# Attention in doubles of two head pairs: tail keys in eight 64x32 tiles, tanh written to SBUF, whole-width loads

## The chip, the core and the metric

The kernel runs on one core of a Trainium2 chip (trn2). A core has five engines with queues of their own: TensorE (PE, with its weight loads shown as PEld), VectorE (DVE), ScalarE (ACT), GpSimd (POOL, here only zeros, ones and stores) and SyncE (SP, which issues loads). They meet through semaphores. SBUF is the working memory of 128 partitions; PSUM, into which PE writes, has eight banks. The metric is the device time of one execution in microseconds (us); less is better.

## What is computed

The reference, cut to what matters (batch 4, 12 heads, 448 positions, head size 64; d_model 768, d_ff 2048; all in fp32):

```python
scores = cap * tanh(q @ k.T / sqrt(64) / cap)          # per batch and head, 448x448
attn = exp(scores - max) / (sum(exp(scores - max)) + 1e-9)
x = heads_side_by_side(attn @ v)                       # 1792 x 768
for w_in, w_out in ((moe_w_in, moe_w_out), (moe2_w_in, moe2_w_out)):
    h = maximum(x @ w_in, 0)
    x = (h * h) @ w_out
```

## The kernel before

The program has two stages. **Attention** works on 24 pairs of heads (batch b, pair j, two heads e = 0, 1), in the order of `PAIRS`. **Four passes** then do the two layers, two batches at a time (passes 0 and 1 layer one, 2 and 3 layer two), as products of 2x2 blocks with seven products instead of eight (names A11, A12, S3, S2, S1, S4, A22). A pass has 56 chunks of six 128x128 weight tiles; per tile three PE products run (L674 to L676: high and low part of weight and input). Each chunk needs its weights loaded (`wf`, issued by SP), their high part (`wh`, ACT) and low part (`wl`, DVE); there are three buffers of each.

In between, DVE and ACT prepare the weights: the inputs are float64 words, which `round_words` turns into float32 one unit at a time (load `ww`, scaled on ACT at L217, then shift L220, low bits L223, sign L226 on DVE; POOL stores `w32`); after two units four block sums (L249) are made and stored in `sums`. This work is spread over attention and passes by due times, at a rate per place (`room`).

Scores stand with keys on partitions and queries along the row. The 448 keys of a head are three tiles of 128 and a rest of 64. A **round** below is a group of matmuls that fill the array side by side. Of one pair:

- scores: three rounds (L336), each of two 64x128 matmuls, one per head, in the two row halves of the array; and one for the rest (L330): four 128x32 matmuls over both heads, where the input `qk` holds zeros so that each head sees its own half;
- ACT: tanh in PSUM (L348) and exp to SBUF (L352), in `GROUPS` of three blocks, three blocks and the rest: 1344, 1344 and 448 columns;
- sums of the weights: two rounds (L382, `ones` as the stationary operand) into bank 7; DVE turns them (L392), adds eps (L399), takes reciprocals (L400) and spreads them (L404);
- values: four rounds (L372) of four 128x32 matmuls into bank 6; DVE multiplies by the reciprocals (L422) into `m` (kept, batches 0 and 1, then split by `bring` into the `xc` slots, ACT line L474) or `o` (stored to memory, batches 2 and 3).

Scores use banks 0 to 2 and 3 to 5 in turn. PE's order in a pair is: scores of pair n, sums and values of pair n-1, rest of pair n. A pair's inputs come by five DMAs: `raw` (two of 64 partitions, three buffers) and `vr` (three; 576 columns that hold a column block of ones beside each head's values, and two strips of 16 KB; three buffers).

The order of every engine is fixed when the program is written: `Plan.emit` is a list scheduler that holds costs, places (one place is 3.66 us of PE time), due times and rings of buffers, and each engine then runs its list in that order, waiting where it has to.

## Time and profile before

| what | us |
|---|---|
| median of 3 runs (1045.92 to 1048.86) | 1046.26 |
| the profiled execution | 1043.62 |
| its span (first to last instruction) | 1041.9 |
| PE busy in the span (98%) | 1019.5 |
| DVE busy (80%) | 834.3 |
| ACT busy (67%) | 698.8 |
| first matmul of attention | 4.70 |
| first matmul of pass 0 | 201.18 |

The profiled execution's own time is 1043.62 us, 1.7 us more than its span and 2.6 us less than the median. The last two lines divide the span: 4.7 us of start, 196.5 us of attention, 840.7 us of passes and last stores.

### The profile page before, as it was taken

The numbers are of one execution on the slowest core, as the hardware profiler recorded it, in microseconds if no ns is written. First come the engines' busy times: TensorE is split into PE (matmuls) and PEld (weight loads), VectorE is DVE, ScalarE is ACT, GpSimd is POOL, SyncE is SP. The second block draws the span as 40 slices with busy tenths as digits, with TensorE's granted clock in tenths as the row PEclk, the third lists the DMA queues.
The fourth block names the chain that finished last, engine by engine and source line by source line (L and its number), as shares of the span: only waits on it lengthen the run. The fifth ranks groups of instructions, "written<-read, shape, count | busy, mean of one in ns | idle before, by whom it ended". The sixth has DMA issues, their size and how long they took to land.

```text
span 1041.9 us, 16113 instructions
## 1 busy us (share of the span) xinstructions
PE 1019.5 (98%) x5664; PEld 826.9 (79%) x5664; DVE 834.3 (80%) x1204; ACT 698.8 (67%) x963; POOL 106.6 (10%) x185
## 2 busy tenths in 40 slices
PE   7999999899999999999999999998999999999997
PEld 3333333499899989899999998987999999999996
DVE  3789877778899999887999988778997865589751
ACT  7999999587786655676965557777565444465541
POOL 0101122112111011111100111210100000000000
PEclk9999999999999999999999999999999999999999
DMA  8989999889885686899746958886646533334341
GB/s 211 295 239 271 294 273 343 287 291 292 287 271 162 211 313 222 279 311 298 252 137 219 320 195 291 269 264 210 185 136 225 155 110 110 106 110 126 116 141 63
DMA packets 107498, 231.59 MB, mean 222 GB/s; under 512 B 17105, under 2 KB 62417, under 8 KB 107409
## 3 DMA queue, kind: packets, MB, share of 16 engines
q1 hardware_dynamic: 92688, 171.88, 55.1%
q0 software_dynamic: 14720, 58.60, 15.2%
q8 instruction: 46, 0.75, 0.3%
q14 instruction: 44, 0.35, 0.1%
HBM read 166.33 MB, written 64.09 MB: 221 GB/s over the span
## 4 chain that ended last, share of the span: by engine, by line
PE 91%; DVE 3%; DMA 2%; ACT 1%; issue 1%; SPq 0%; DVEq 0%; ACTq 0%
PE bank L676 25%; PE bank L674 25%; PE bank L675 25%; PE bank L372 6%; PE bank L336 5%; PE bank L382 3%; PE bank L330 1%; DMA wf<-si 1%; DMA ww<-wout_dram 1%; DVE wl L189 1%; DVE xc L189 1%; ACT bank L348 1%; ACT p L352 0%; DVE wg L223 0%; DMA raw<-qk_dram 0%
## 5 line engine op out<-in xcount | busy, mean ns | idle before, releaser
L676 PE MATMUL bank<-xc,wl 128*128 128x448 f32 x1344 | 493.1, 367 | 6.8 <-DVE wl L189 6.8
L674 PE MATMUL bank<-xc,wh 128*128 128x448 f32 x1344 | 492.8, 367 | 1.2 <-ACT one L693 1.2
L675 PE MATMUL bank<-xc,wh 128*128 128x448 f32 x1344 | 492.5, 366 | 0.0
L607 ACT ACTIVATE wh<-wf 128x768 fp32r<-128x768 f32 x224 | 187.8, 842 | 175.0 <-PE bank L675 146.0
L676 PEld LDWEIGHTS bank<-xc,wl 128*128 128x128 f32 x1344 | 252.9, 188 | 30.8 <-DVE wl L189 9.0
L189 DVE TENSOR_TENSOR wl<-wf,wh 128x768 fp32r<-128x768 f32 x224 | 212.0, 953 | 80.6 <-ACT wh L607 79.7
L674 PEld LDWEIGHTS bank<-xc,wh 128*128 128x128 f32 x1344 | 252.9, 188 | 24.4 <-ACT one L693 1.6
L675 PEld LDWEIGHTS bank<-xc,wh 128*128 128x128 f32 x1344 | 252.9, 188 | 21.7
L693 ACT ACTIVATE one<-bank 128x448 f32<-128x448 f32 x132 | 71.1, 539 | 63.4 <-PE bank L676 58.5
L348 ACT ACTIVATE bank<-bank,caps 128x1344 f32<-128x1344 f32 (+1 forms) x72 | 79.3, 1102 | 9.1 <-PE bank L336 7.0
L352 ACT ACTIVATE p<-bank,caps 128x1344 f32<-128x1344 f32 (+1 forms) x72 | 81.6, 1133 | 2.2
L695 DVE TENSOR_TENSOR one<-bank,one 128x448 f32<-128x448 f32 x96 | 59.0, 621 | 27.2 <-PE bank L676 23.2
L372 PE MATMUL bank<-p,vr 128*32 128x448 f32 x768 | 76.6, 539 | 0.8 <-DVE o L422 0.8
L217 ACT ACTIVATE wg<-ww 128x768 f32<-128x768 f32 (+1 forms) x68 | 58.7, 866 | 17.3 <-DMA ww<-wout_dram 10.6
L336 PE MATMUL bank<-raw 64*128 64x448 f32 x288 | 64.7, 570 | 5.4 <-DMA raw<-qk_dram 4.7
L372 PEld LDWEIGHTS bank<-p,vr 128*32 128x32 f32 x768 | 24.9, 110 | 48.3 <-issue 44.0
L223 DVE SCALAR_TENSOR_TENSOR wg<-ww,wg 128x768 uint32<-128x768 uint32 (+1 forms) x68 | 61.8, 908 | 1.7
L226 DVE SCALAR_TENSOR_TENSOR wg<-ww,wg 128x768 uint32<-128x768 uint32 (+1 forms) x68 | 61.6, 906 | 1.4
L336 PEld LDWEIGHTS bank<-raw 64*128 64x128 f32 x288 | 28.3, 192 | 41.0 <-issue 22.3
L220 DVE TENSOR_SCALAR wg<-wg 128x768 uint32<-128x768 uint32 (+1 forms) x68 | 36.1, 530 | 15.7 <-ACT wg L217 15.7
L189 DVE TENSOR_TENSOR xc<-ga,xc 128x896 fp32r<-128x896 f32 (+1 forms) x50 | 45.5, 917 | 2.4 <-ACT xc L535 2.3
L382 PE MATMUL bank<-p,ones 128*32 128x448 f32 x384 | 41.1, 545 | 1.8 <-ACT p L352 1.8
(80 smaller groups left out, 815.7 us busy)
## 6 DMA issues: line engine op xcount, KB each, us to landing
wf<-si SPq DMA_DIRECT2D x120, 192.0 KB, 4.3
ww<-wout_dram SPq DMA_DIRECT2D x24, 768.0 KB, 7.4
wf<-wi SPq DMA_DIRECT2D x96, 192.0 KB, 3.8
ww<-win_dram SPq DMA_DIRECT2D x64, 192.0 KB, 5.9
wi<-wg POOLq DMA_DIRECT2D x32, 384.0 KB, 6.0
si<-wg POOLq DMA_DIRECT2D x32, 384.0 KB, 4.7
ww<-win_dram SPq DMA_DIRECT2D x16, 768.0 KB, 6.5
wf<-so SPq DMA_DIRECT2D x32, 384.0 KB, 3.5
```

What stands on the lines that cost most here:

```text
L189: nc.vector.tensor_tensor(out, a, b, op=ALU.subtract)
L223: nc.vector.scalar_tensor_tensor(m["fu"], m["t"][:, :n, 0], 29, m["fu"], op0=ALU.logical_shift_right, op1=ALU.bitwise_or)
L336: nc.tensor.matmul(groups_of[n][gi]["s"][:, at], lhsT=stk["t"][rows, S + 128 * t:S + 128 * t + 128], rhs=stk["t"][rows, :S], start=True, s ...
L348: nc.scalar.activation(s["s"], s["s"], AF.Tanh, scale=rcap)
L352: nc.scalar.activation(s["p"], s["s"], AF.Exp, scale=capt)
L372: nc.tensor.matmul(bank[32 * z:32 * z + 32, 6, :S], lhsT=vt["t"][:, w:w + 32], rhs=weights(n, t, e), start=t == 0, stop=t == 3)
L382: nc.tensor.matmul(bank[32 * z:32 * z + 32, 7, :S], lhsT=ones[:, 1 + e if t == 3 else 0], rhs=weights(n, t, e), start=half == 0, stop=half ...
L607: nc.scalar.activation(m["hi"], m["f"], AF.Copy)
L674: nc.tensor.matmul(a, lhsT=hi, rhs=x(0), start=first and z == 0, stop=False, skip_group_check=more)
L675: nc.tensor.matmul(a, lhsT=hi, rhs=x(1), start=False, stop=False, skip_group_check=more)
L676: nc.tensor.matmul(a, lhsT=lo, rhs=x(0), start=False, stop=final and z == len(xs) - 1, skip_group_check=more)
L693: nc.scalar.activation(m[g, i, n], a, AF.Copy)
```

## The change

Pairs are taken two at a time, as 12 **doubles** (u = 0, 1). Per double:

- scores: six rounds of two 64x128 matmuls (now L354; cells of two banks: 0-1, 2-3, 4-5), and one round for the rests of both pairs (L361): eight 64x32 matmuls, one per pair, head and 32 keys, in both row halves and all four column strips of the array. Each column strip writes one bank from one row half and another bank from the other; each of the two banks is written from both row halves, at different partitions;
- ACT: tanh from PSUM to SBUF (L367), 896 columns, seven times; exp in place in SBUF (L373) over 2, 2 and 3 rounds (1792, 1792, 2688 columns). The weights of a double are one tile of seven rounds, `pe` for even and `p` for odd doubles;
- sums: four rounds (L416) into one of the score cells; one turn (L426), six small operations (L431, L434, L435) and one spread of 896 columns (L439) on DVE;
- values: six rounds (L393) of four 128x32 matmuls into banks 6 and 7, and one round (L405) of eight 64x32 for the rests; one multiplication of 896 columns (L458).

`raw` is one DMA of 128 partitions per pair (four buffers). `vr` is 448 columns without the ones, by four DMAs in runs of 512 and 256 bytes (four buffers). The first units' `ww` load is one DMA instead of four. The scaling of units due in attention moves from ACT to DVE (L228). The block A21 of the rounded weights, which only the branch for a wide `cap` reads, is no longer stored; that branch makes it itself. The `wf`, `wh` and `wl` buffers take the space of `pe` and are opened after double 10's last values (`open_w`). The rates at which units are spread over the passes change (`RATES`).

```diff
-GROUPS = [[("A", 0), ("B", 0), ("A", 1)], [("B", 1), ("A", 2), ("B", 2)], [("R", 3)]]
-PARTS = [(slice(32 * r, 32 * r + 32), slice(32 * z, 32 * z + 32)) for z, r in enumerate((0, 2, 1, 3))]
+KV = 448
+EXPS = {None: [(0, 2), (2, 4), (4, 7)], 0: [(0, 1), (1, 3), (3, 5), (5, 7)], 11: [(0, 2), (2, 4), (4, 6), (6, 7)]}
...
-STEP = 2.14
-T0 = -STEP * (len(PAIRS) + 0.7)
+DOUBLES = len(PAIRS) // 2
+STEP = 3.76
+T0 = -STEP * (DOUBLES + 0.62)
+SWITCH = 0
+RATES = (1.5, 1.7, 0.5, 1.2, 0.8, 1.6)
+IN = 1.05
-URGENT = 2.0
+URGENT = 0.5
...
-    w_hi = [wp.tile([128, KC, 128], F32R, name=f"wh{i}") for i in range(3)]
-    w_f = [wp.tile([128, KC, 128], F32, name=f"wf{i}") for i in range(3)]
-    w_lo = [wp.tile([128, KC, 128], F32R, name=f"wl{i}") for i in range(3)]
+    even = ExitStack()
+    p_even = even.enter_context(tc.tile_pool(name="pe", bufs=1)).tile([128, 7, 2, S], F32, name="pe")
+    w_f, w_hi, w_lo = [], [], []
...
-            for rows, own in PARTS if l == g == 0 else [(slice(0, 128), slice(0, 128))]:
-                nc.sync.dma_start(to[own], src[rows])
+            nc.sync.dma_start(to, src)
+
+        on_act = t0 > SWITCH
...
-            nc.scalar.activation(m["ff"], m["t"][:, :n, 1].bitcast(F32), AF.Copy, scale=2.0 ** -112)
+            words = m["t"][:, :n, 1].bitcast(F32)
+            if on_act:
+                nc.scalar.activation(m["ff"], words, AF.Copy, scale=2.0 ** -112)
+            else:
+                nc.vector.tensor_scalar(m["ff"], words, 2.0 ** -112, None, op0=ALU.mult)
...
-            nc.gpsimd.dma_start(w32[l, g, i][:, :, c0:c1], m["f"][:, :2 * (c1 - c0)].rearrange("p (h c) m -> p h c m", h=2))
+            h0 = int(lower_half)
+            nc.gpsimd.dma_start(w32[l, g, i][:, h0:, c0:c1], m["f"][:, h0 * (c1 - c0):2 * (c1 - c0)].rearrange("p (h c) m -> p h c m", c=c1 - c0))
...
+        lower_half = i >= (HC if g else HF)
...
+    def open_w():
+        even.close()
+        pool = ctx.enter_context(tc.tile_pool(name="w2", bufs=1, reuse_waits="tile"))
+        for to, n, dt in ((w_f, "wf", F32), (w_hi, "wh", F32R), (w_lo, "wl", F32R)):
+            to.extend(pool.tile([128, KC, 128], dt, name=f"{n}{i}") for i in range(3))
+
     def attention():
-        groups_of, vt_of, stk_of = [], [], []
-        v_of = [qkp.tile([128, VL], F32, tag=f"vr{i}", name="vr", bufs=1) for i in range(3)]
+        p_of = [p_even, pp.tile([128, 7, 2, S], F32, tag="p", name="p", bufs=1)]
+        v_of = [qkp.tile([128, KV], F32, tag=f"vr{i}", name="vr", bufs=1) for i in range(4)]
...
+                raw["t"] = qkp.tile([128, QW], F32, tag="raw", name="raw", bufs=4)
+                nc.sync.dma_start(raw["t"], qk[b, 2 * j:2 * j + 2].rearrange("h r w -> (h r) w")[64:192])
+
+            def load_v():
+                t, src = v_of[vt["at"][0]], v[b, j]
+                nc.sync.dma_start(t[:, 64:320].rearrange("p (t w) -> p t w", w=128), src[:, 128:512].rearrange("p (t w) -> p t w", w=192)[:, :, :128])
+                nc.sync.dma_start(t[:, :384].rearrange("p (t w) -> p t w", w=64)[:, 0:6:5], src[:, :576].rearrange("p (t w) -> p t w", w=64)[:, 0:9:8])
+                for e in range(2):
+                    nc.sync.dma_start(t[half(e ^ u), 384:], src[half(e), 576 + 192 * e:640 + 192 * e])
+        def scores(k, r, place, cost):
...
+                at = cell[0]
+                if r < 6:
+                    t, w = raw_of[k, us[0]]["t"], S + 128 * (r % 3)
...
+                        nc.tensor.matmul(bank[:, at + e, :S], lhsT=t[half(e), w:w + 128], rhs=t[half(e), :S], start=True, stop=True)
+                    return
+                for u in us:
+                    t = raw_of[k, u]["t"]
+                    for z in range(4):
+                        e = z // 2 ^ u
+                        w = S + 384 + 64 * e + 32 * (z % 2)
+                        nc.tensor.matmul(bank[32 * z:32 * z + 32, at + u, :S], lhsT=t[half(e), w:w + 32], rhs=t[half(e), :S], start=True, stop=True)
+
+            o = pe(cost, emit, place, [raw_of[k, u]["done"] for u in us], take=[("sc", cell)], drop=["raw"] * 2 if r == 6 else [])
+            due = start(k) + 0.45 * r
+
+            def tanh():
+                nc.scalar.activation(p_of[k % 2][:, r], bank[:, cell[0]:cell[0] + 2, :S], AF.Tanh, scale=rcap)
+
+            p_set[k, r] = op("ACT", 978, tanh, due, [o], take=[f"p{k % 2}{r}"], drop=[("sc", cell)])
+
+        def exps(k, lo, hi, due):
+            def exp():
+                nc.scalar.activation(p_of[k % 2][:, lo:hi], p_of[k % 2][:, lo:hi], AF.Exp, scale=capt)
...
+        def values(k, r, place, cost, first, final, **more):
...
+                    e, h = z // 2, z % 2
+                    w = 128 * t + 64 * e + 32 * h
+                    nc.tensor.matmul(bank[32 * z:32 * z + 32, 6 + u, :S], lhsT=vt_of[k, u]["t"][:, w:w + 32], rhs=p_of[k % 2][:, r, e],
+                                     start=first, stop=final, skip_group_check=True)
+
+            return reads(k, [r], emit, place, cost, [vt_of[k, u]["done"]], **more)
+
+        def tails(k, place, cost, first, **more):
             def emit():
+                for u in range(2):
+                    for z in range(4):
+                        e, h = z // 2, z % 2
+                        rows = half(e ^ u)
+                        w = 384 + 32 * h
+                        nc.tensor.matmul(bank[32 * z:32 * z + 32, 6 + u, :S], lhsT=vt_of[k, u]["t"][rows, w:w + 32], rhs=p_of[k % 2][rows, 6, u],
+                                         start=first, stop=not first, skip_group_check=True)
+
+            return reads(k, [6], emit, place, cost, [vt_of[k, u]["done"] for u in range(2)], **more)
...
+                        z = 2 * e + u
+                        rhs = p_of[k % 2][:, 3 * u + t, e] if t < 3 else p_of[k % 2][:, 6, u]
+                        nc.tensor.matmul(bank[32 * z:32 * z + 32, cell[0], :S], lhsT=ones[:, 0 if t < 3 else 1 + (e ^ u)], rhs=rhs,
+                                         start=first, stop=final, skip_group_check=True)
...
+                nc.vector.tensor_scalar(m["q"], t.unsqueeze(1).to_broadcast([128, 2, S // 32]), eps, None, op0=ALU.add)
+                for z in range(4):
+                    to, own = (slice(32 * y, 32 * y + 32) for y in (z, z ^ 1))
+                    nc.vector.tensor_scalar(m["q"][to, 1 - z % 2], t[own], eps[own], None, op0=ALU.add)
...
+                nc.vector.tensor_tensor(to, bank[:, 6:8, :S], r["r"], op=ALU.mult)
...
+        def order(k):
+            new, old = [("S", r) for r in range(7)] if k < DOUBLES else [], []
+            V, D = [("V", r) for r in range(6)], [("D", t) for t in range(4)]
+            if k == 0:
+                return new
+            if k == 1:
+                return new[:2] + V[:3] + new[2:3] + V[3:] + D[:3] + new[3:] + [("T", 0), D[3]]
+            if k == DOUBLES:
+                return V[:2] + V[3:5] + D[:2] + [V[2], V[5]] + D[2:] + [("T", 0)]
+            return new[:3] + D + new[3:] + [("T", 0)] + V
...
+                if k - 1 == last - 1:
+                    pe(0, open_w, at, drop=[(n, [i]) for n in ("wf", "wh", "wl") for i in range(3)])
...
-                room += 0.5 * (1.5 if at_place < 0 else 1.4 if at_place % 56 < 28 else 0.6)
+                room += 0.5 * RATES[0 if at_place < 0 else min(int(at_place // 28) + 1, 5)]
...
-        plan.emit({"ww0": 1, "ww1": 1, "wg": 4, "wf": 3, "wh": 3, "wl": 3, "sc": [0, 3], "pv": 1, "p3": 4, "p1": 2,
-                   "raw": 3, "vr": 3, "d": 1, "y": 2, "dn": [7], "rn": 2, "o": 3, "m0": 1, "m1": 1,
+        plan.emit({"ww0": 1, "ww1": 1, "wg": 4, "wf": [], "wh": [], "wl": [], "sc": [0, 2, 4], "pv": 1, **{f"p{e}{r}": 1 for e in range(2) for r in range(7)},
+                   "raw": 4, "vr": 4, "d": 1, "y": 2, "rn": 1, "o": 2, "m0": 1, "m1": 1,
...
```

PE's list, from the middle of attention (x counts matmuls; `p`, `pe`: the weights exp(tanh)). Before, one pair:

```order
L330 MATMUL bank<-raw 32x448 x4
L336 MATMUL bank<-raw 128x448 x6
L382 MATMUL bank<-p,ones 32x448 x8
L372 MATMUL bank<-p,vr 32x448 x16
L330 MATMUL bank<-raw 32x448 x4
```

and now, one double:

```order
L354 MATMUL bank<-raw 128x448 x6
L416 MATMUL bank<-pe,ones 32x448 x16
L354 MATMUL bank<-raw 128x448 x6
L361 MATMUL bank<-raw 32x448 x8
L405 MATMUL bank<-pe,vr 32x448 x8
L393 MATMUL bank<-pe,vr 32x448 x24
```

A pair had 10 rounds, so two had 20; a double has 18, and it goes from one shape of tile to another five times instead of four.

ACT's list there. Before, a rest and the six blocks of the next pair, with one split of `bring` and one scaling of weights between:

```order
L348 ACTIVATE bank<-bank,caps 128x448
L352 ACTIVATE p<-bank,caps 128x448
L474 ACTIVATE xc_211<-m_228 128x448
L348 ACTIVATE bank<-bank,caps 128x3x448
L352 ACTIVATE p<-bank,caps 128x1344
L348 ACTIVATE bank<-bank,caps 128x3x448
L352 ACTIVATE p<-bank,caps 128x1344
L217 ACTIVATE wg_230<-ww_234 128x768
```

and now, one double's tanh and exp and the start of the next:

```order
L367 ACTIVATE pe<-bank,caps 128x896 x2
L373 ACTIVATE pe<-pe,caps 128x1792
L367 ACTIVATE pe<-bank,caps 128x896 x2
L373 ACTIVATE pe<-pe,caps 128x1792
L367 ACTIVATE pe<-bank,caps 128x896 x3
L373 ACTIVATE pe<-pe,caps 128x2688
L367 ACTIVATE p<-bank,caps 128x896 x2
```

Two pairs were 12 instructions, a double is 10, over the same 12,544 columns; no scaling of weights is left between them.

DVE's list where attention ends. Before, the first two low parts of weights (`wl`) stand ahead of the last three pairs' sums:

```order
L422 TENSOR_TENSOR o<-bank,rn 128x448
L189 TENSOR_TENSOR wl_242<-wf_239,wh_236 128x768
L189 TENSOR_TENSOR wl_243<-wf_240,wh_237 128x768
L392 STREAM_TRANSPOSE tn<-bank 128x448
L399 SCALAR_TENSOR_TENSOR dq<-tn,eps 64x14 x2
L400 RECIPROCAL dq<-dq 128x14
```

and now:

```order
L458 TENSOR_TENSOR o<-bank,rn 128x896
L240 SCALAR_TENSOR_TENSOR wg_233<-ww_235,wg_233 128x768
L243 SCALAR_TENSOR_TENSOR wg_233<-ww_235,wg_233 128x768
L228 TENSOR_SCALAR wg_230<-ww_234 128x512
L237 TENSOR_SCALAR wg_230<-wg_230 128x512
L240 SCALAR_TENSOR_TENSOR wg_230<-ww_234,wg_230 128x512
L243 SCALAR_TENSOR_TENSOR wg_230<-ww_234,wg_230 128x512
L195 TENSOR_TENSOR wl_1667<-wf_1661,wh_1664 128x768
L426 STREAM_TRANSPOSE tn<-bank 128x448
L195 TENSOR_TENSOR wl_1668<-wf_1662,wh_1665 128x768
```

The turn of the last double's sums stands behind the first low part, and that behind the first load of `wf`.

## Rows read from the trace of the kernel before

**Rows 1.** Busy time by stretch (start:end us, length, engines, PEclk, DMA share, GB/s).

```profile
26.00:170.00 144.00, 144.00 (x1254) 50.97 (x1246) 117.01 (x224) 138.07 (x140) 19.74 (x36) 1.00 0.98 283
201.00:1035.00 834.00, 826.00 (x4034) 757.58 (x4031) 682.87 (x914) 515.77 (x777) 77.20 (x123) 1.00 0.65 211
```

**Rows 2.** Chain that ended last, in attention (start us, us, what; xN rows).

```profile
20.73 2.46 PE bank L336 x12
23.19 1.64 PE bank L382 x16
24.83 3.01 PE bank L372 x32
27.84 0.75 PE bank L330 x8
...
169.98 2.48 PE bank L336 x12
```

**Rows 3.** The same chain at the start of attention.

```profile
4.70 3.37 PE bank L336 x6
8.09 1.36 ACT bank L348
```

**Rows 4.** PE in order of time where pass 0 begins.

```profile
201.18 0.47 PE L674 MATMUL bank<-xc,wh 128*128 128x448 f32 x1
```

**Rows 5.** ACT in 20:170 by shape (count, busy us, mean ns, idle before us).

```profile
L352 ACT ACTIVATE p<-bank,caps 128x1344 f32<-128x1344 f32 x38 | 52.5, 1383 | 1.1
L348 ACT ACTIVATE bank<-bank,caps 128x1344 f32<-128x1344 f32 x38 | 51.3, 1351 | 2.2 <-PE bank L336 2.2
L352 ACT ACTIVATE p<-bank,caps 128x448 f32<-128x448 f32 x19 | 12.1, 635 | 0.6
L348 ACT ACTIVATE bank<-bank,caps 128x448 f32<-128x448 f32 x19 | 11.5, 606 | 2.1 <-PE bank L330 2.1
L474 ACT ACTIVATE xc<-m 128x448 fp32r<-128x448 f32 x15 | 8.3, 567 | 0.0
```

**Rows 6.** ACT in order of time (start us, us of one, instruction).

```profile
163.86 1.35 ACT L348 ACTIVATE bank<-bank,caps 128x1344 f32<-128x1344 f32 x1 [0.39 <-PE bank L336]
165.25 1.38 ACT L352 ACTIVATE p<-bank,caps 128x1344 f32<-128x1344 f32 x1
166.52 1.35 ACT L348 ACTIVATE bank<-bank,caps 128x1344 f32<-128x1344 f32 x1
```

**Rows 7.** DVE in 20:170 by shape (columns as in rows 5).

```profile
L392 DVE STREAM_TRANSPOSE tn<-bank 128x448 f32<-128x448 f32 x19 | 12.3, 646 | 17.2 <-PE bank L382 13.7 <-ACT p L352 3.5
...
L220 DVE TENSOR_SCALAR wg<-wg 128x768 uint32<-128x768 uint32 x17 | 9.3, 547 | 0.4 <-ACT wg L217 0.4
L399 DVE SCALAR_TENSOR_TENSOR dq<-tn,eps 64x14 f32<-64x14 f32 x38 | 9.1, 240 | 0.9
...
L422 DVE TENSOR_TENSOR m<-bank,rn 128x448 f32<-128x448 f32 x12 | 7.4, 621 | 2.6 <-PE bank L372 2.4
```

**Rows 8.** DMA: one queue's packets (MB, share), issues (count, KB, us to landing).

```profile
q1 hardware_dynamic: 92688, 171.88, 55.1%
...
wf<-si SPq DMA_DIRECT2D x120, 192.0 KB, 4.3
...
raw<-qk_dram SPq DMA_DIRECT2D x48, 240.0 KB, 5.1
...
vr<-v_dram SPq DMA_DIRECT2D x24, 288.0 KB, 5.1
...
vr<-v_dram SPq DMA_DIRECT2D x48, 16.0 KB, 4.6
```

**Rows 9.** Chain that ended last, at the end of attention (columns as in rows 2).

```profile
176.29 9.09 DMA wf<-si
```

**Rows 10.** Groups by line, the whole span (columns as in rows 5).

```profile
L189 DVE TENSOR_TENSOR wl<-wf,wh 128x768 fp32r<-128x768 f32 x224 | 212.0, 953 | 80.6 <-ACT wh L607 79.7
L607 ACT ACTIVATE wh<-wf 128x768 fp32r<-128x768 f32 x224 | 187.8, 842 | 175.0 <-PE bank L675 146.0 <-issue 20.5 <-ACT xc L535 3.3
```

## What the change should do to the time

> **What bounds the kernel now.** First the busy time by stretch [rows 1]: from 26 to 170 us, inside attention, PE is busy for all of 144.00 us, ACT for 138.07 and DVE for 117.01. From 201 to 1035 us, the passes, PE is idle for 8.0 of 834 us. PE sets the time in both stages, so a gain has to come from less PE work in attention, and ACT, at 96%, stands close behind. Next the chain in order of time [rows 2]. Of one pair it holds three score rounds in 2.46 us, two sum rounds in 1.64, four value rounds in 3.01 and the rest in 0.75: 7.86 us. The next such 2.46 begins 149.25 us later after 19 pairs, so a pair takes 7.855 us and nothing but PE is in it. A value round is 3.01 / 4 = 0.7525 us. Three of these would be 2.26, and two 1.505: the change of tile shape into the scores costs 0.20 us and the one into the sums 0.135; between sums and values, of one shape, it costs nothing. Ten rounds and 0.335 us are the pair. Attention runs from 4.70 to 201.18 us [rows 3, 4], 196.5 us: 24 pairs are 188.5, and 8.0 go to filling and draining.
>
> **The steady double.** Two pairs cost 15.71 us. A double has 18 rounds, 13.545 us, and five changes of shape: values to scores 0.20, scores to sums 0.135, sums to scores 0.20, and two that the trace doesn't show, into and out of 64x32. For these I take 0.135 each, the row for going into a shape 32 columns wide; the ends are 0 (sums to values) and 0.20. Sum: 0.805, a double 14.35 us (14.08 to 14.48), 1.36 less than two pairs. This takes an eight-tile round at the price of a four-tile one. The trace shows two row halves at once (the scores) and four column strips at once (the values), each at 0.75 a round, and never both; the other bounds are under the rivals.
>
> The Trainium skill, TensorE: Matmul & The Clock Gate, section Measured speedup vs the span model, would make eight tiles one matmul's time plus some 4 ns a tile: by it, an estimate, 0.03 us more a round and under 1 us in all. No run here shows it.
>
> **Does ACT hold 14.35?** A tanh of 896 columns lies between 606 ns at 448 and 1351 at 1344: 978 [rows 5]. An independent instruction starts 1.27 us after one of 1.38 us, a dependent one 1.39 after one of 1.35 [rows 6], so the pitch of tanh is 0.90 and exp pays 0.03 for waiting. Exp is 1.76 us for 1792 columns and 2.51 for 2688, on the line through 635 and 1383. Sum: 7 x 0.90 + 2 x 1.76 + 2.51 + 0.1 = 12.4 us. The 15 splits [rows 5] at 0.49 net come three to a double in five doubles: 13.9. Exp and tanh of one size differ there by 0.03, which is the price I see for writing SBUF instead of PSUM; on all ten instructions it makes 14.2 in those five doubles. ACT fits, and only just. Within a double the walk is: S0 to S2 end at 2.5 us, the sums take a cell when the first tanh is done at 2.0, end at 5.6, the turn frees that cell at 6.4; S3 to S5 end at 8.1 and S5 wants that cell at 7.3; the rests want the cell of the fourth tanh, done at 7.6, at 8.1. The slack is 0.9 and 0.5 us. DVE stands at 81% [rows 1]; per double it loses 5.3 us of two pairs' small work (646, two at 240 and a reciprocal of the same 14 columns, 646 for the spread, 621) and gets 4.3 (646, six small ones at 240, and two of 896 columns, 1.1 each) [rows 7]. The scaling that it takes over is 0.55 a unit, by the like step, at 17 units in 11 doubles, 0.9. That cancels the gain, and ACT, which gave it up, no longer waits for `ww`. SP's list gets six fewer issues for the first units and three more a double for `vr`; bytes fall: two pairs moved 960 KB of `raw`, 640 of `vr` and 17 units in 150 us of 1536 KB each (768 read, 384 stored as `w32`, 384 of sums), 4330 KB; a double moves 960, 448 and 1.55 units of 1440, 3630 KB, or 259 GB/s against the 283 of rows 1.
>
> **Start.** One `raw` DMA of 240 x 2 KB instead of two [rows 8]; the first half's matmuls stood at 4.70, and I put the first round at 5.3. The first two rounds took 3.37 us [rows 3], so the first now ends at 6.7 and tanh begins at 6.8, 1.3 earlier than before. From there ACT is the bound: double 0 (four exps) takes 12.7 us, to 19.5. Of double 1 the two first rounds wait for cells until 17.8, then nine rounds and a score round keep PE to 25.8, while ACT has run dry at 23.9; S3 ends at 26.7, ACT needs 8.3 us more to finish double 1, at 35.0, and PE, held by the cells, starts double 2 at 33.1. Its sums want a cell that the next tanh frees at 36.0, 0.4 late.
>
> **End.** Doubles 2 to 11: 33.1 + 0.4 + 10 x 14.35 = 177.0. The last step is 11 rounds and one change, 8.4 us, to 185.4. Now the weights: their first load can't start before 177.0, since its space is `pe`. SP's issue 0.7, a load of 4.3 (median) or 9.1 us (the one on the chain) [rows 8, 9], `wh` 0.84, `wl` 0.95 [rows 10]: 183.8 or 188.6. The first is hidden by the last step, the second is 3.2 late and also holds the last turn on DVE, behind `wl`. At 4.3 it costs nothing, and the row is nearer to it, since `ww` traffic is no denser; I add 0.5. Pass 0 begins at 185.9 instead of 201.2: **15.3 us**.
>
> **Passes.** PE's list is the same there, and 8.0 us of idleness [rows 1] are what can change. DVE's and ACT's weight work is laid out anew: 21 units ahead of the first chunk instead of 18, so less in pass 0, but runs of about 9 us of DVE work between two `wl` (a chunk is 3.66) stand now at chunk 27 and near 31, 114 and 116, as they did at 48, 60 and 139. I count 0, with -6 and +6 as ends. A21's stores save only DMA.
>
> Sum against the profiled execution: 1043.6 - 15.3 = 1028.3. That execution is 2.6 below the median, so **1031** for a median.
>
> **Rivals.** (a) *The eight tiles don't run at once.* For: no row shows it, and each bank of such a round is written from both row halves. If the round falls into two groups of four, it costs 0.75 more, twice a double: 18.1 us in twelve, and the gain is gone: 1049, 0.26% over before. If only the low halves of one group meet the high halves of the other, 0.376 once a double, 4.5 us: 1035. Against: each strip writes two different banks, as the score rounds do.
>
> The Trainium skill, TensorEngine Tiling (Array Packing), section Gotcha 1: PSUM Pressure, speaks against this change: different row tiles cannot access one PSUM bank at the same time. By it the time would be that of the two groups. The trace has only rounds that keep to the rule, so no row weighs it.
>
> (b) *DMA takes PE's place, and the time is over that of before.* Its place is 26 to 180 us, where the DMA share is already 0.98 [rows 1]. `vr` goes from 512 packets a double to 1280. A packet of the issuing queue takes 0.551 x 16 x 1041.9 / 92688 = 0.099 us of one engine [rows 8]; at that price 768 more are 4.7 us of all sixteen, and the double, 0.98 x 15.71 x 3630 / 4330 = 12.9 now, would need 17.6 us: 12 x 3.3 = 39 more, 1070. It binds from 30 ns a packet and makes the kernel slower than before from 57. What fails then is `ww`: DVE's list waits for it ahead of a turn, the turn holds a cell, PE stops. Against: a strip of 64 short packets lands in 4.6 us beside 5.1 for 288 KB [rows 8].
>
> (c) *Attention gains, the passes give most of it back.* The late load (3.2), ACT a little over in five doubles (2) and three more DVE runs of 9 us (6): 1042. For: DVE is busy for 82% of the passes. Against: before had such runs too.
>
> **How the numbers follow.** A measurement can tell 0.3%, 3.1 us, from no change. Chances: the forecast 0.70, by itself 1023 to 1038; (a) 0.09, half of it in each form; (b) 0.07; (c) 0.14. Range 1021 to 1043: below, -6 in the passes, both changes of shape free (-2.7) and a start 1 us shorter; above, (c). Outside are (a) in full, (b), and a rest at both ends. Faster by over 0.3% (under 1043.1): 0.70, half of (a), most of (c), less a rest: 0.86. Within: (a) in full and the end of (c), 0.07. Slower: (b), 0.07.
>
> **What would show it.** In the profile after, the chain should hold score rounds 14.3 to 14.5 us apart, six 64x32 rests in 0.75 to 0.8 us; over 1.1 means (a). PE idle inside attention with `tn` or `ww` as releaser means (b). Pass 0 should begin near 186 us with less than 1 us of waiting for `wl`; the idle time of PE in the passes should be 2 to 14 us. Were the pitch of tanh 1.18 us or more, (14.35 - 12.4) / 7 over my 0.90, PE would wait for ACT in every double, and the forecast would be wrong by its own ACT term.

## The result, and the profile after

Nine executions of the changed kernel have a median of 1037.55 us (1031.2 to 1044.27), nine of the kernel before on the same chip 1046.36. The ratio is 0.991, with a 95% interval of 0.9883 to 0.9936: faster, 6.5 us above the forecast of 1031 and inside its range. The profiled execution took 1032.11 us (span 1030.3), 11.5 less than that of before.

The starts of the passes' 4032 matmuls divide this. A distance from one start to the next of over 0.6 us is a gap, one of 0.24 to 0.6 us a slow matmul, and the rest is steady; of the first two, what is over 203 ns is counted.

| stretch | before | after | difference | predicted |
|---|---|---|---|---|
| up to the first matmul of pass 0 | 201.18 | 193.97 | -7.2 | -15.3 |
| passes, steady | 822.3 | 817.5 | -4.8 | 0 |
| passes, slow matmuls | 2.6 | 2.6 | 0 | 0 |
| passes, gaps of PE | 9.1 | 9.6 | +0.5 | 0, from -6 to +6 |
| behind the last matmul's start, and around the span | 8.4 | 8.4 | 0 | 0 |

So half of attention's gain is missing, and there is one that nobody had forecast. The table holds for the two profiled executions; in a second trace of the changed kernel (run again, below) the steady part is 824.9 us, 2.6 more than before, so the 4.8 is not the kernel's in every execution. The chain of one steady double of after, which answers to [rows 2]:

```profile
51.45 2.46 PE bank L354 x12
53.91 3.14 PE bank L416 x32
57.05 2.46 PE bank L354 x12
59.51 0.91 PE bank L361 x16
60.42 0.75 PE bank L405 x16
61.17 4.65 PE bank L393 x48
65.82 2.46 PE bank L354 x12
```

A double takes 65.82 - 51.45 = 14.37 us (forecast 14.35), and nothing but PE is in it. The value rests, eight 64x32 tiles, take 0.75 us, what four tiles take; the score rests take 0.91, with 0.16 for the change of shape. Work by stretch, which answers to [rows 1], with two lines of the page on DMA (the last 11 us of the second stretch lie behind the passes' last matmul, at 1023.73, so its idle time is not that of the gaps):

```profile
26.00:170.00 144.00, 140.42 (x1304) 48.39 (x1304) 125.47 (x225) 130.35 (x114) 23.76 (x39) 0.99 0.78 254
201.00:1035.00 834.00, 814.36 (x3999) 751.39 (x3997) 683.49 (x910) 512.50 (x773) 73.88 (x121) 0.99 0.63 204
450.00:600.00 150.00, 150.00 (x742) 139.00 (x741) 136.93 (x174) 101.73 (x151) 17.48 (x31) 1.00 0.73 243
```

```profile
DMA packets 114919, 222.92 MB, mean 216 GB/s; under 512 B 22480, under 2 KB 73744, under 8 KB 114832
q1 hardware_dynamic: 101136, 169.52, 52.6%
```

In attention ACT has room now (130.35 of 144, from 138.07), DVE is at 87%, and the DMA share fell from 0.98 to 0.78 although the issuing queue moves 8448 packets more [rows 8]. Below, step n is PE's work from the first score round of double n to that of double n + 1, and the last step is what follows the values of double 10. Now the start, as PE went through it, and the DVE row behind which DVE's work piles up (it has no pause from there to 40.7 us):

```profile
28.17 1.02 PE L354 MATMUL bank<-raw 64*128 64x448 f32 x4 [0.36 <-ACT p L367]
30.89 1.75 PE L361 MATMUL bank<-raw 64*32 64x448 f32 x16 [1.69 <-ACT p L367]
32.38 1.75 PE L405 MATMUL bank<-pe,vr 64*32 64x448 f32 x16
34.06 0.97 PE L416 MATMUL bank<-pe,ones 128*32 128x448 f32 x8
34.97 2.90 PE L354 MATMUL bank<-raw 64*128 64x448 f32 x12
...
44.12 1.02 PE L354 MATMUL bank<-raw 64*128 64x448 f32 x4 [1.40 <-DVE tn L426]
```

```profile
27.86 0.56 DVE L228 TENSOR_SCALAR wg<-ww 128x768 f32<-128x768 f32 x1 [7.07 <-DMA ww<-win_dram]
```

and the end, with the DVE rows of that time below it:

```profile
176.34 4.72 PE L393 MATMUL bank<-pe,vr 128*32 128x448 f32 x48
183.69 4.91 PE L393 MATMUL bank<-p,vr 128*32 128x448 f32 x32 [2.63 <-DVE o L458]
188.41 1.69 PE L416 MATMUL bank<-p,ones 128*32 128x448 f32 x16
```

```profile
181.48 0.56 DVE L228 TENSOR_SCALAR wg<-ww 128x768 f32<-128x768 f32 x1 [0.31 <-DMA ww<-wout_dram]
182.07 0.56 DVE L237 TENSOR_SCALAR wg<-wg 128x768 uint32<-128x768 uint32 x1
182.55 1.08 DVE L458 TENSOR_TENSOR o<-bank,rn 128x896 f32<-128x896 f32 x1
```

Two waits that weren't in the sum: at 44.12 for a turn, and at 183.69 for the product of the double before, since the last step begins with value rounds, which want its banks; that product stood on DVE's list behind two unit steps, the first of which waited for its load. The wait of 1.69 us for tanh, at 30.89, was in the sum: the prediction let PE be held by the cells up to 33.1. But this gap and that of 2.63 us are paid twice. The windows of that time (the last three columns are granted clock, DMA share, GB/s):

```profile
31.00:33.00 2.00, 2.00 (x24) 0.57 (x32) 1.93 (x4) 0.97 (x2) 0.89 (x1) 0.50 0.57 120
33.00:35.00 2.00, 2.00 (x26) 0.21 (x10) 1.93 (x4) 1.97 (x2) 0.40 (x1) 0.71 0.93 280
...
184.00:186.00 2.00, 2.00 (x16) 0.56 (x12) 1.46 (x2) 0.00 (x0) 1.26 (x3) 0.58 1.03 392
186.00:188.00 2.00, 2.00 (x16) 0.64 (x12) 0.85 (x2) 0.80 (x1) 0.33 (x1) 0.56 1.04 388
```

Behind the gaps of 1.69 and 2.63 us PE ran at or near 0.50, the level of 1.2 GHz: the rests took 1.75 us in place of 0.98, four value rounds 4.91 in place of 3.2.

### The profile page after: what moved, and what is told of

It reads as the page before. It is cut to its first block, busy times and chain, and to the rows that moved or that the text cites. A ratio compares the mean times of both kernels' runs of the same rounds, so it can differ in the third digit from the quotient of the medians.

```text
span 1030.3 us, 15832 instructions
## 1 busy us (share of the span) xinstructions
PE 1001.5 (97%) x5664; PEld 819.5 (80%) x5664; DVE 839.4 (81%) x1191; ACT 676.6 (66%) x918; POOL 105.9 (10%) x179
## 4 chain that ended last, share of the span: by engine, by line
PE 90%; DVE 4%; DMA 4%; issue 1%; SPq 0%; POOL 0%; ACT 0%; DVEq 0%; POOLq 0%
PE bank L751 25%; PE bank L749 25%; PE bank L750 25%; PE bank L393 5%; PE bank L354 4%; PE bank L416 3%; DMA ww<-win_dram 1%; DVE wg L272 1%; PE bank L361 1%; PE bank L405 1%; DMA ww<-wout_dram 1%; DMA raw<-qk_dram 1%; DMA si<-wg 1%; DMA wo<-wg 1%; DVE wl L195 0%
## 5 line engine op out<-in xcount | busy, mean ns | idle before, releaser
L354 PE MATMUL bank<-raw 64*128 64x448 f32 x288 | 64.7, 578 | 8.4 <-DMA raw<-qk_dram 4.8
L354 PEld LDWEIGHTS bank<-raw 64*128 64x128 f32 x288 | 26.5, 194 | 46.0 <-issue 25.5
L367 ACT ACTIVATE p<-bank,caps 128x896 f32<-128x896 f32 x42 | 40.3, 998 | 11.2 <-PE bank L354 10.1
L367 ACT ACTIVATE pe<-bank,caps 128x896 f32<-128x896 f32 x42 | 40.3, 1002 | 7.7 <-PE bank L354 7.7
L226 ACT ACTIVATE wg<-ww 128x768 f32<-128x768 f32 (+1 forms) x45 | 38.0, 847 | 6.1 <-DMA ww<-wout_dram 4.1
L195 DVE TENSOR_TENSOR xc<-gb,xc 128x448 fp32r<-128x448 f32 (+1 forms) x52 | 38.7, 763 | 2.0 <-ACT xc L610 1.2
L272 DVE TENSOR_TENSOR wg<-wg,wg 128x384 f32<-128x384 f32 (+1 forms) x68 | 36.3, 534 | 2.2
L373 ACT ACTIVATE p<-p,caps 128x1792 f32<-128x1792 f32 (+2 forms) x19 | 37.0, 1949 | 0.6
```

The source lines that it names most:

```text
L195: nc.vector.tensor_tensor(out, a, b, op=ALU.subtract)
L354: nc.tensor.matmul(bank[:, at + e, :S], lhsT=t[half(e), w:w + 128], rhs=t[half(e), :S], start=True, stop=True)
L367: nc.scalar.activation(p_of[k % 2][:, r], bank[:, cell[0]:cell[0] + 2, :S], AF.Tanh, scale=rcap)
```

## The experiments

Times are medians; ratios are against the kernel before, run with them.

**Again** (no edit).

> The changed kernel once more, with no edit, since its times lie 13 us apart where those of the kernel before lie 5 apart. If the spread is in the first or the last doubles (waits for a `ww` load, and slow rounds behind them), this trace has pass 0 beginning at another time than 193.97 us, and the passes as long as in the trace shown (829.8 us from their first matmul to their last). If it is in the passes, pass 0 begins within 0.5 us of 193.97 and the sum of PE's gaps there, 10.3 us, changes instead. Either way a steady double is 14.37 us.

Median 1033.16 us, ratio 0.9872 (0.9836 to 0.9909). The profiled execution took 1041.61. Its windows:

```profile
31.00:33.00 2.00, 2.00 (x40) 0.55 (x38) 1.90 (x5) 1.73 (x2) 0.24 (x1) 1.00 1.01 249
```

```profile
450.00:600.00 150.00, 150.00 (x727) 136.27 (x727) 134.21 (x170) 102.10 (x151) 17.06 (x31) 1.00 0.73 243
750.00:900.00 150.00, 150.00 (x742) 139.13 (x741) 109.53 (x148) 74.37 (x109) 0.00 (x0) 1.00 0.47 146
```

Both halves of the expectation fell. Pass 0 began at 192.54, 1.4 earlier: after the same wait of 1.7 us the clock stayed at 1.00 this time. The gaps were as before (9.7 us). What differs is the steady part, 824.9 against 817.5 us: 727 matmuls in 150 us instead of 742, that is 206.67 ns apart (mean over hundreds of starts), up to the gap at 637 us but for 12 us from 298 on, and 202.67 from there on. Slow matmuls take another 3.5 us; most of them stand 373 to 374 ns apart behind a gap, as from 637 to 642 us, where the granted clock is 0.50. So this execution lost its 9.5 us in the steady part and the slow matmuls; PE's gaps don't show it, and the granted clock of the steady part is 1.00. The other executions left no trace; that the long ones among them lose their time in the same way is likely, and not shown.

**Rest4**: the eight tiles undone in one place.

```diff
-lhsT=t[half(e), w:w + 32], rhs=t[half(e), :S]
+lhsT=t[:, w:w + 32], rhs=t[:, :S]
```

> The eight 64x32 matmuls of the last 64 keys become eight 128x32, so that two follow each other in each column strip (they contract over the rows of both heads, so those scores are not the reference's). This undoes the eight tiles at once in one of the two places and nothing else. Theory: the round of eight costs what a round of four costs, so the edit costs one round of 0.75 us a double, with the changes of shape 0.6 to 0.95: a double of 15.0 to 15.3 us, and 12 doubles are 7 to 11 us slower than the changed kernel. Rival: the eight tiles run as two groups of four already, and nothing changes (a double of 14.37).

```profile
55.66 2.46 PE bank L354 x12
58.12 1.64 PE bank L361 x16
...
70.92 2.46 PE bank L354 x12
```

The rests take 1.64 us instead of 0.91, the double 70.92 - 55.66 = 15.26, 0.89 more. Median 1041.64, ratio 0.9957 (0.9937 to 0.9978); against the unedited kernel of again, run beside it (0.9872), that is by the ratios 8.9 us more, within the 7 to 11 expected. Eight tiles in the two halves and four strips do run at once; one such round is worth 0.89 us a double, and two at that price, an estimate, are 1.78, more than the whole 1.36 that a double gained.

**Sums_first**: the last step begins with sums (in PE's lists V stands for a value round, D for a sum round, T for the value rests, `new` for the score rounds).

```diff
-return V[:2] + V[3:5] + D[:2] + [V[2], V[5]] + D[2:] + [("T", 0)]
+return D[:3] + V + D[3:] + [("T", 0)]
```

> The order of PE's last step alone: three sum rounds, then the six value rounds, the last sum round and the rests, in place of value rounds first. Theory on the end: in the changed kernel the first value round of the last step waits 2.63 us for the product of the double before (its banks), and the clock granted after that gap is near half for four rounds, 1.9 us. With three sum rounds in front, 2.3 us of other work cover the gap: under 0.7 us of waiting, rounds at 0.75 us, and pass 0 begins 3.5 to 4.5 us earlier, near 190 us. Rival: the weights of pass 0 are late too (`wl` ends at 190.3 us), or the last turn and the last product are what pass 0 needs: it begins no earlier than 192.

```profile
183.15 4.72 PE L393 MATMUL bank<-p,vr 128*32 128x448 f32 x48 [0.40 <-DVE o L458]
...
189.55 0.44 PE L749 MATMUL bank<-xc,wh 128*128 128x448 f32 x1
...
191.89 0.70 PE L751 MATMUL bank<-xc,wl 128*128 128x448 f32 x1 [1.70 <-DVE wl L195]
```

The gap is covered, the clock holds, and pass 0 begins 4.4 us earlier than in the first trace of after and 3.0 earlier than in the second. The starts differ too; from the first scores of double 11 to pass 0 it takes 23.50 us here (from 166.05), 27.35 and 27.17 in the two traces, so the end itself gains 3.7 to 3.9. But the median is 1042.94 us, ratio 0.9942 (0.9919 to 0.9965): the third matmul waits for `wl`, which stands behind the last turn on DVE, and two more gaps come at 283 and 290 us (3.0 and 1.1 us), behind a `ww` load of 9.8 us and a `wf` load of 4.9. The gain was as expected, and the passes took 10 us more than in the first trace of after.

**Step1**: score round 3 goes ahead of six others in the second step.

```diff
-return new[:2] + V[:3] + new[2:3] + V[3:] + D[:3] + new[3:] + [("T", 0), D[3]]
+return new[:2] + V[:3] + new[2:4] + V[3:] + D[:3] + new[4:] + [("T", 0), D[3]]
```

> The order of PE's second step alone: score round 3 of double 1 goes ahead of value rounds 3 to 5 and the three sum rounds. Theory on the start: ACT ran dry for 2.83 us there, since that score round stood behind six other rounds; PE then waited 1.69 us for tanh, and the granted clock fell to 0.50 for the next rounds, some 1.5 us more. With the round ahead ACT goes on, the gap goes and the clock stays at 1.00: step 2 begins at 31 to 32 us instead of 34.97. If DVE's list, whose units stand ahead of the first turn and wait for a `ww` load until 27.9 us, doesn't come in its place, step 3 begins 3 to 4 us earlier than 51.4; the rival is that it does, with the turn at about 34 us as the releaser of PE's next gap, and step 3 begins at 49.5 to 51.4.

```profile
30.61 0.99 PE L361 MATMUL bank<-raw 64*32 64x448 f32 x16 [0.36 <-ACT p L367]
...
33.17 2.53 PE L354 MATMUL bank<-raw 64*128 64x448 f32 x12
36.25 3.21 PE L416 MATMUL bank<-p,ones 128*32 128x448 f32 x32 [0.56 <-ACT pe L367]
```

The wait of 1.69 us is 0.36; step 3 begins at 48.16, 3.2 us earlier than in the first trace of after and 2.0 earlier than in the second. No turn was waited for; the `ww` load, which DVE's list awaits ahead of the first turn, landed at 25.2 us here, and at 27.9 and 26.9 in the two traces of after. Step 2 began at 33.17, later than expected: the rounds behind the first gap, at 17 us, were slow here (three value rounds 3.42 us for 2.46). Median 1034.35, ratio 0.9894 (0.9856 to 0.9932). The unedited kernel of again, run beside it, has 0.9872 (0.9836 to 0.9909): the time shows no gain. Two later runs with this order (step1_laid and both_laid, below) had the load at 27.9 and 27.7 us, and a turn held PE:

```profile
35.87 1.86 PE L354 MATMUL bank<-raw 64*128 64x448 f32 x4 [2.62 <-DVE tn L426]
...
50.26 2.53 PE L354 MATMUL bank<-raw 64*128 64x448 f32 x12
```

These are step1_laid's; both_laid has a wait of 2.50 us and step 3 at 50.15, the second trace of after 50.17. So the rival holds in two of three traces, and the 2.0 us came with the early load.

**Rates**: the table of before in the passes.

```diff
-RATES = (1.5, 1.7, 0.5, 1.2, 0.8, 1.6)
+RATES = (1.5, 1.4, 0.6, 1.4, 0.6, 1.4)
```

> The changed kernel with the kernel before's table of how many weight units are laid out to each stretch of the passes; attention's work is as changed. What this tests is the prediction's term for the passes, zero with 6 us either way. A walk down DVE's list with the durations of the trace (0.95 us for a step over 768 columns, 0.56 for the like half-rate steps, 0.94 for `wl`, a chunk of PE 3.65 us, three `wl` buffers) gives PE 11.9 us of gaps for the changed kernel (chunks 28, 31, 114, 116; measured 12.8) and 38.7 for this one (most at chunks 36 to 39 and at 143, 14.7 by itself). Theory: gaps of 25 to 40 us in the passes and a time of 1045 to 1060 us, slower than the kernel before. Rival: the buffers hide such runs, and the time stays within 6 us of the changed kernel's.

What PE waited for in the passes (us in total, times, longest):

```profile
PE bank L749 <- ACT wh L682: 16.8, 4, 11.0
PE bank L751 <- DVE wl L195: 12.5, 10, 2.2
```

1065.79 us, above the 1045 to 1060 expected, ratio 1.0223 (1.0183 to 1.0263), with 32.6 us of gaps and 11.7 of slow matmuls. With attention as changed and the old table the change would have been a loss.

**Act_scale**: the scaling back on ACT.

```diff
-SWITCH = 0
+SWITCH = -1000
```

> The first step of every weight unit, the scaling, goes back from DVE to ACT; nothing else is edited. From 26 to 170 us ACT is busy for 130.4 of 144 us in the changed kernel and DVE for 125.5; 15 to 16 scalings of 0.87 to 0.90 us make ACT 144.4 and DVE 116.7. Theory: ACT then bounds the doubles that also hold splits, PE waits for tanh or exp there, the doubles with splits take 14.7 to 15.3 us instead of 14.37, and pass 0 begins 2 to 6 us later than in the changed kernel. Rival: since ACT only has to keep the mean, the doubles stay at 14.37 and pass 0 begins within 1 us of 192.5 to 194.

```profile
26.00:170.00 144.00, 138.83 (x1290) 47.35 (x1288) 116.13 (x206) 139.83 (x127) 20.43 (x37) 1.00 0.78 259
```

```profile
183.75 3.21 PE L393 MATMUL bank<-p,vr 128*32 128x448 f32 x32 [1.21 <-DVE o L458]
```

ACT does get in the way: from step 3 to the last double's scores, eight doubles, it takes 118.94 us (49.15 to 168.09), 14.87 a double, instead of 115.20 (50.17 to 165.37) in the second trace of after. But the gap ahead of the last step is 1.21 us and the clock holds behind it (3.21 us for four value rounds), so pass 0 began at 192.34, no later. I had not seen that the same edit takes work from DVE ahead of that product: here DVE waited 2.67 us for the values before it. Median 1049.01, ratio 1.003 (1.0 to 1.0061): 14.3 us of gaps in the passes, 9.3 of slow matmuls, and 206.67 ns from 643 us on.

**Before_again, before_moved, before_pad**: where the steady distance comes from. Moved:

```diff
     xp = ctx.enter_context(tc.tile_pool(name="xp", bufs=1))
+    wq = ctx.enter_context(tc.tile_pool(name="wq", bufs=1))
...
-    w_hi = [wp.tile(
+    w_hi = [wq.tile(
```

and so for `w_f` and `w_lo`; `w_f` now stands ahead of `w_hi`, and `xc` and `m` move down by the 27 KB a partition that the nine buffers took. Padded:

```diff
+                        for _ in range(2 if n == t == e == 0 else 1):
                             nc.tensor.matmul(groups_of[n][gi]["s"][:, at],
```

> The kernel before, with no edit, for a second trace. Three distances between matmuls of the passes stand in the traces so far, each held for hundreds of matmuls, with changes only at a gap of PE: 204.0 ns all through the first trace of the kernel before, 202.67 all through the changed kernel's, 206.67 up to a gap at 637 us and 202.67 after it in that kernel's second. If the distance belongs to the kernel, this trace has 204.0 everywhere; if it belongs to the execution and is drawn anew at gaps, other levels stand here too, and the time follows them with 4.03 us for each nanosecond over all 4032 matmuls.

> The kernel before with one edit: the nine buffers of `wf`, `wh` and `wl` are put in SBUF behind `xc` and `m`, where the changed kernel has them, in place of ahead of them; no instruction is added, removed or moved. In both traces of the kernel before the passes' matmuls stand 204.00 ns apart from first to last, through gaps of PE and all; in every trace of the changed kernel and its variants they stand 202.67 or 206.67 apart. Theory 1: the place of weights and data in SBUF sets the level; this run shows 202.67 or 206.67 like the changed kernel, and at 202.67 it is 5.4 us faster than the kernel before with the work the same (a time near 1040). Theory 2: the number of instructions ahead on PE sets it; this run stays at 204.00 and at 1046.

> The kernel before with one matmul more: the first score matmul of the first pair is issued twice, so that all later instructions of PE stand one matmul and one weight load further on. Theory 2 of the run beside it (the count of instructions ahead): the distance of the passes' matmuls leaves 204.00 ns. Theory 1 (the place in SBUF): it stays at 204.00 everywhere, and the time is that of the kernel before, 1044 to 1049.

The windows of before_again, then of before_moved:

```profile
450.00:600.00 150.00, 150.00 (x737) 138.11 (x736) 135.70 (x172) 106.24 (x159) 17.12 (x30) 1.00 0.76 254
```

```profile
300.00:360.00 60.00, 60.00 (x292) 54.51 (x291) 57.09 (x67) 37.75 (x52) 5.54 (x9) 1.00 0.63 200
450.00:600.00 150.00, 150.00 (x742) 139.00 (x741) 136.10 (x174) 105.31 (x158) 17.20 (x30) 1.00 0.77 257
```

Before_again (1048.38 us) and before_pad (1045.64), one execution each, stand at 204.00 ns throughout. Before_moved stands at 202.67 up to 254 us, 206.67 up to a gap at 381, and 202.67 from there on; its steady part is 819.4 us, its median 1043.97, ratio 0.9979 (0.9963 to 0.9996). So the place of the buffers in SBUF, of the weights and with them of `xc` and `m`, decides whether the matmuls stand 204.00 apart or on one of the other two distances; which of the buffers matters, no run separates. The mean hides a rhythm: at 204.00 five distances repeat (200, 209, 196, 203, 212 ns at 460 us in before), at 202.67 nearly five (about 203, 199, 207, 202, 203 in after), and at 206.67 all are 206 or 207 (again). Why place sets it, and what picks between 202.67 and 206.67, stays open: most changes come at a gap of PE, but before_moved went to 206.67 at 254 us, and after and step1_laid back to 202.67 at 650 and 699 us, with no gap there.

**Turn_first**: no unit but the first two may start ahead of the first two turns.

```diff
-round_block(l, g, i, k, due - 8, 2.4, due)
+round_block(l, g, i, k, due - 8 if l == g == i == 0 else max(due - 8, T0 + 14 + 2 * i), 2.4, due)
```

> In the changed kernel the weight units after the first two may start later, so that none stands on DVE's list ahead of the first two turns (the order of PE is as in the changed kernel). It tests the other suspect for the late start: in the changed kernel's two traces PE waited 1.40 us, and 0.64 and 1.17 us, for a turn behind units whose `ww` load landed at 27.9 us. Theory: these waits go and step 3 begins 1.2 to 1.8 us earlier than with the same rounds before it (51.4 in the slower of the two traces, 50.2 in the other); the wait of 1.7 us for tanh at 30.9 us stays, since that one is ACT's. The units come later: the walk down DVE's list gives 18.7 us of gaps in the passes (5.5 at the first chunks, 4.5 at 31) where the changed kernel's gives 11.9, so the time should be 3 to 7 us above the changed kernel's all the same. Rival: the loads of that time are short of DMA bandwidth, and the first turns wait as long without units ahead.

```profile
32.68 0.99 PE L361 MATMUL bank<-raw 64*32 64x448 f32 x16 [1.69 <-ACT p L367]
...
38.32 3.21 PE L416 MATMUL bank<-p,ones 128*32 128x448 f32 x32 [0.56 <-ACT pe L367]
...
181.58 3.21 PE L393 MATMUL bank<-p,vr 128*32 128x448 f32 x32 [1.21 <-DVE o L458]
```

From the rest round at 32.68 to step 3 at 50.23 it took 17.55 us, in the second trace of after 19.28 (30.89 to 50.17): the waits for turns, 1.8 us, are gone, and ACT's stays. Pass 0 began at 190.14, with the short gap at the end too. The passes lost it all, with 19.4 us of gaps: 1047.01 us, ratio 1.0015 (0.9992 to 1.0037), by the ratios 11 us above the first nine executions of the changed kernel for the 3 to 7 expected: against the first trace of after the gaps rose by 9.8 us where the walk had 6.8, and slow matmuls behind them, which the walk doesn't have, by 6.3.

**Step1_laid and both_laid**: the better orders with a table chosen by the walk.

```diff
-RATES = (1.5, 1.7, 0.5, 1.2, 0.8, 1.6)
+RATES = (1.5, 1.8, 0.4, 1.3, 0.6, 1.6)     # step1_laid
+RATES = (1.6, 1.9, 0.3, 1.2, 0.8, 1.4)     # both_laid
```

> The order of PE's second step as in the run step1, and another layout of the weight units over the passes, chosen by the walk down DVE's list: 7.0 us of gaps (chunks 49, 115, 116, 118, 148) where the changed kernel's gives 11.9. If the walk holds, the gaps in the passes fall from 12 to 13 us to 7 to 9, and the time by 4 us against step1: 1026 to 1031 with matmuls 202.67 ns apart. Rival: waits for loads of `ww`, which the walk doesn't see, fill the difference, and it is no faster than step1.

> Both orders of PE (second step as in step1, last step as in sums_first) and a layout of the weight units for which the walk down DVE's list gives 5.0 us of gaps (chunks 27, 49, 114 to 116). If the gains add, step 3 begins at 48.2 us, pass 0 at 186 to 188 (190.3 in step1, less 2 to 4.4 for the gap ahead of the last step), the passes have 6 to 9 us of gaps, and the time is 1021 to 1027 with matmuls 202.67 ns apart. Rival, from the run sums_first: what the end gains is taken back by the first chunks, since `wl` of chunk 1 and the units of pass 0 were late by as much (1.9 us at chunk 0, 2.97 and 1.11 at chunks 24 and 25): no faster than step1_laid, 1026 to 1031.

Step1_laid: 1029.48 us (1025.63 to 1041.86), as expected, ratio 0.984 (0.9814 to 0.9866), the best that was run; its interval lies below that of the changed kernel's first nine executions and overlaps that of again (0.9836 to 0.9909). Its passes hold 8.2 us of gaps and 1.4 of slow matmuls. The start gave nothing: the turn at 36 us held PE, and pass 0 began at 192.38, as in again (192.54). Both_laid: 1040.3 us for the 1021 to 1027 expected, ratio 0.9935 (0.991 to 0.996). Its profiled execution was the longest of six (1049.55), and 12.2 us of what it has over the first trace of after is steady distance, most of it at 206.67 ns. Pass 0 began at 188.5, and then, from 189 to 310 us, DVE waited:

```profile
DVE one L770 <- PE bank L751: 15.3, 8, 3.1
```

against 5.1 us in after: it stood idle for results of PE in front of unit work, and PE then for `wl`. The walk takes DVE as never idle and misses this. That these waits made the gaps is argued from the order of the lists; no run removes them. How the walk did (us; a dash where none is on record):

| kernel | gaps by the walk | gaps | slow matmuls | steady |
|---|---|---|---|---|
| after | 11.9 | 9.6 | 2.6 | 817.5 |
| step1_laid | 7.0 | 8.2 | 1.4 | 818.1 |
| turn_first | 18.7 | 19.4 | 8.9 | 817.7 |
| rates | 38.7 | 32.6 | 11.7 | 818.4 |
| sums_first | – | 15.5 | 5.8 | 818.7 |
| both_laid | 5.0 | 17.4 | 5.5 | 829.7 |

## Why the prediction was right and where it was wrong

- **The steady double: right.** 14.37 us for 14.35. The changes of shape sum to 0.83 (0.20, 0.13, 0.20, 0.16, 0.135) for the 0.805 assumed, and rival (a) is out by rest4. The Trainium skill, TensorEngine Tiling (Array Packing), section Gotcha 1: PSUM Pressure, forbids one bank to two row tiles at a time. Here two row tiles write one bank at different partitions, and the round takes 0.75 us, what a round within the rule takes. The measurement decides: the rule doesn't bind in this case.
- **ACT and DMA: right in the steady doubles.** Tanh ran at 1.00 us for the 0.978 assumed. Its pitch, 0.90, is what was measured (three in a row took 2.79 us, the last 1.00), though the rows that the prediction gives for it make it 0.87 (0.978 less 1.38 - 1.27). Act_scale shows that with the scaling at its old place ACT would have cost 0.47 us a double. Rival (b) is out as a rate: packets rose, the DMA share fell. Its last link (DVE's list waits for `ww` ahead of a turn, the turn holds a cell, PE stops) did happen, once at the start, and is the next item.
- **The start: mis-sized by 3.6 us** (step 3 at 51.4 for 47.85; 2.3 in the second trace). The prediction had step 2 at 33.1; the second trace has 33.45. What failed is "Its sums want a cell that the next tanh frees at 36.0, 0.4 late": turns held PE, for 1.40 us in the first trace and 1.81 in the second, behind units that DVE could start only when their load landed, at 27.9 and 26.9 us. Turn_first, without these units there, has no such wait. In the first trace the low clock cost 1.5 us more ahead of step 2, which the prediction doesn't have. Step1's order doesn't remove the turn's wait when the load is late.
- **The end: wrong by 4** (23.25 us forecast from the first scores of double 11 to pass 0, 27.35 measured). "The last step is 11 rounds and one change, 8.4 us" took the last step as joined to the one before. Its first rounds need banks that DVE must empty first: 1.2 us at the least (act_scale, turn_first), 2.63 with a unit ahead of that product, and about 1.7 more at the low clock. Sums_first takes 23.50 us for the same stretch. The load of `wf`, on which the prediction dwelt, was in time only because pass 0 was late: in after the first `wh` waited for it to 187.20 us and the first `wl` ended at 190.3, for 183.8 forecast. With pass 0 at 189.55 and 188.52, in sums_first and both_laid, the third matmul waited 1.7 us for `wl`.
- **The passes: a zero made of two.** The gaps were as said, +0.5, at or beside the chunks named (28, 31, 114, 116). That the range of 6 us stood for any layout was wrong: the old table costs 33 us more in the passes, so the new table is a part of the change without which it loses. And the steady distance gave 4.8 us in the first trace and took 2.6 in the second, from buffers that moved only to make room for `pe`. The prediction held that PE's list is the same there; it is, and runs at another pace.
- **The median.** It was forecast as 2.6 us above the profiled execution, as before; it stood 5.4 above. The likely reason: the changed kernel's traces fall on 202.67 or 206.67 ns (16 us apart over all 4031 distances, and its nine times span 13) and those of before, three with the padded one, on 204.00.

In sum: -7.2 where -15.3 was expected, and -4.8 that no term held. The runs account for the missing 8.1 (3.6 at the start, 0.4 in the doubles between, 4.1 at the end); of the 4.8 they show what sets it, the place of the buffers, and not how. That the time came out within 7 us of the forecast is in part luck: without the 4.8 the profiled execution would be 6.7 us faster than before, not 11.5, and the second trace, without that gain, is only 2.0 faster.

## What to carry to other kernels

Walk the seams, where one stage's last step meets the next: there a product that frees a bank, and whatever stands ahead of it on its engine, has no cover, and a PE gap is often paid again in slow matmuls. When buffers move, compare the steady distance between matmuls before comparing waits. A gain at one seam can be lost behind it, where the work is still due when it was: of four kernels whose trace began pass 0 before 191 us, three lost it again in the passes, and a new layout chosen without DVE's idle time didn't keep it (both_laid). And compare an edit with the unedited kernel run beside it, in more than one trace: step1's gain at the start was gone in two of three.

## What the hardware showed that was not expected

- The same list of matmuls ran at three steady distances, 202.67, 204.00 and 206.67 ns, at a granted clock of 1.00, each held over hundreds of matmuls; the two outer ones changed into each other, mostly at gaps. Where the buffers lie decides between 204.00 and these two (before_moved). The Trainium skill, SBUF — State Buffer, section SBUF: two separate sides, says that PE never waits at its ports. No run here shows a port; place does change PE's pace.
- At the end of attention the clock stayed behind gaps of 1.2 and 1.3 us (act_scale, turn_first, rest4: four value rounds in 3.21 us), and behind gaps of 2.2 to 2.6 us the same rounds took 4.82 to 4.91 (five traces). Behind gaps of 1.7 us it went either way: at 31 us it fell to 0.50 in one of seven traces, at 17 us to between 0.50 and 0.68 in two of nine. The same kernel can differ by 1.5 us from this alone.
